# Strided attention's q and k loaded by strips of 36 partitions and turned as blocks of 108 rows, q and k weights split by expert, the last output tile in halves, and a new order of all operations

## The chip, the cores and the metric

The kernel runs on one core of a Trainium2 chip. The metric is the device time of one execution in microseconds, as the median of several runs. Beside it one execution was taken by the hardware profiler; its trace gives the span from the first to the last instruction and what every engine did in it.

## The reference

Sparse attention with eight heads is followed by a mixture of four causal attention experts of which each token uses two. Everything is float32; the weights of q and k of the experts are drawn eight times larger than the listing shows.

```python
# attention: q, k, v are [8 batches, 8 heads, 576, 64]
scores = scale * np.matmul(q, k.transpose(0, 1, 3, 2))
mask_local = (rel >= 0) & (rel < 32)                       # heads 0 to 3
mask_strided = (rel >= 0) & (pos[None, :] % 32 == pos[:, None] % 32)   # heads 4 to 7
attn = softmax(scores where the head's mask holds)
x = heads side by side of attn @ v                          # [8, 576, 512]
# mixture: wq, wk, wv are [4, 512, 64], wo is [4, 64, 512]
logits = x @ w_gate                                         # the two largest experts, softmax of the two
for e in range(4):
    q, k, v = x @ wq[e], x @ wk[e], x @ wv[e]
    a = causal softmax of scale * (q @ k.T)
    out += weight of e (0 where not chosen) * (a @ v @ wo[e])
```

## The kernel before

The work of a batch has two stages. Stage 1 takes two heads at a time, so a batch has two local pairs (heads 0 to 3) and two strided pairs (heads 4 to 7). It loads q, k and v, turns q and k so that the head dimension lies on the partitions (`tp`, then copies `tp_out` out of PSUM into the tile `qkt`), takes the scores (L633 local, L649 strided), masks them, runs a softmax in six steps spread over VectorE, GpSimd and ScalarE, turns the result (L703 or L713), multiplies by v (L743 local, L762 strided), and splits the attention output into a rounded part `xh` and a remainder `xl`. Stage 2 projects these to q, k and v of the experts with three float32r matmuls per product (L913, L925 for the first pair of experts of batch 0, L860 for v), and goes on with causal scores (L971), softmax, transposes (L1070), values (L1109) and the output projection `out_tile` (L1138).

Batches 0 and 1 turn q and k on TensorE; from batch 2 on (`quad`) VectorE does it. For a strided pair of batches 0 and 1, a token's place is 32 j + g with residue g; L506 loads each strip of 11 or 10 residues on 18 partitions (j) with both heads beside each other, q from partition 0 and k from partition 64 of the tile `nat`, and L603 turns pieces of 54 rows, q and k on two halves of the array. `nat` has three buffers, `qkt` two.

The weights are split into a rounded part and a remainder, `hi_w` on ScalarE and `lo_w` on VectorE or GpSimd. For q and k they are loaded and split by slice of 128 inputs, all four experts in one piece, so any projection needs all four pieces of its weight.

The program is a list of operations (`OPS`) with their dependences. A written table decides the rest: `ORDER` is the sequence in which the operations are issued, and so the sequence on every engine's queue; `SECOND` says which operations run on the second of their two possible engines; `FILL` puts filler matmuls ahead of an operation, if a PSUM bank is free then:

```python
for n, i in enumerate(ORDER):
    o = OPS[i]
    e = list(o.eng)[i in SECOND]
    if o.fill and RB.first() is not None:
        bank = RB.tiles[RB.first()]
        for _ in range(o.fill):
            nc.tensor.matmul(bank[:, :128], ident, ident, start=True, stop=True)
    o.fn(e)
```

Five more matmuls, `warm`, stand first on TensorE (L1158). All loads and stores are issued by SyncE's queue in the table's sequence.

Of the kernel before, what the change touches and what calls it, by code (L numbers as in the profile page):

```python
# [20 lines left out]
def attention_moe_kernel(  # L21
# [20 lines left out]
    nc = tc.nc  # L42
# [38 lines left out]
    class Ring:  # L81
# [34 lines left out]
    }  # L116
    ORDER = [
# [1103 lines left out]
```

## Time and profile before

| | before |
|---|---|
| median of 3 runs (lowest to highest) | 439.55 us (439.47 to 440.03) |
| the profiled execution: its time, its span | 439.54 us, 437.8 us |
| TensorE busy | 428.4 us, 98% of the span |
| VectorE, ScalarE, GpSimd busy | 356.3, 268.3, 231.1 us |
| first matmul, first projection (L925), last matmul's copy | 2.57, 42.44, 434.11 us |
| filler matmuls (L304) | 122 records, 18.0 us busy, all before the first projection |
| granted TensorE clock | 1.00 over the span |

Times within the trace count from the start of the span; 1.7 us of the execution's time lie around it. A float32 matmul that is not a transpose has two records, a transpose or a float32r matmul one. A busy TensorE counts fillers as work. An engine that is busy is not for that the one that is waited for: the chain of waits says which was.

### The profile page before, as it was taken

Reading aid. Unit: us, or ns where it says so; the run is one execution under the profiler, and the core shown is the slowest. Engines: PE = TensorE matmul, PEld = TensorE weight load, DVE = VectorE, ACT = ScalarE, POOL = GpSimd, SP = SyncE. Lnnn points to the kernel's source line nnn. Section 1 sums busy time; section 2 is a strip of 40 time slices with the busy share of each in tenths; the row PEclk is TensorE's granted clock in tenths of the full one; section 3 lists DMA queues with packets and bytes.
Section 4 is the critical chain, followed back from the end, with each engine's and each line's share of the span. In section 5 each row is a group of like instructions: output and inputs, shape, how many; then the busy total and the mean of one; then the engine's idle time right before and its main releaser. Section 6 shows DMA issues by size and latency. Waiting matters only on the chain.

```text
span 437.8 us, 18842 instructions
## 1 busy us (share of the span) xinstructions
PE 428.4 (98%) x7588; PEld 376.6 (86%) x7588; DVE 356.3 (81%) x1140; ACT 268.3 (61%) x852; POOL 231.1 (53%) x375
## 2 busy tenths in 40 slices
PE   7999999999999999999999999999999999999996
PEld 6998998997789889788889788998789988998675
DVE  4798999899998896998889888896888888458750
ACT  4486647857676475566665378725577377557743
POOL 4164782678717842843819633679026771417720
PEclk9999999999999999999999999999999999999999
DMA  7665754766635634653256236355241030011113
GB/s 193 155 147 145 144 113 97 148 105 109 125 61 96 122 98 79 137 115 81 51 106 122 76 90 137 73 104 111 73 118 40 1 108 1 26 24 53 70 53 120
DMA packets 156271, 41.87 MB, mean 96 GB/s; under 512 B 145976, under 2 KB 149432, under 8 KB 156184
## 3 DMA queue, kind: packets, MB, share of 16 engines
q1 hardware_dynamic: 156184, 40.67, 42.0%
q8 instruction: 60, 0.98, 0.9%
q14 instruction: 27, 0.22, 0.2%
HBM read 31.20 MB, written 9.44 MB: 93 GB/s over the span
## 4 chain that ended last, share of the span: by engine, by line
PE 86%; DVE 5%; ACT 4%; DMA 2%; issue 1%; SPq 1%; POOL 1%; DVEq 0%; POOLq 0%; ACTq 0%
PE bank L913 19%; PE bank L1138 11%; PE bank L860 10%; PE bank L1109 10%; PE bank L1070 6%; PE bank L971 6%; PE bank L743 3%; PE bank L762 3%; PE bank L304 2%; PE bank L633 2%; PE bank L1008 2%; PE bank L649 2%; PE bank L713 2%; PE bank L925 2%; PE bank L823 1%
## 5 line engine op out<-in xcount | busy, mean ns | idle before, releaser
L1043 POOL TENSOR_SCALAR p<-p,st,wt 128x384 f32<-128x384 f32 (+3 forms) x128 | 77.3, 622 | 42.0 <-DVE st L1034 22.9
L983 ACT ACTIVATE p<-p,st 128x256 f32<-128x256 f32 (+3 forms) x128 | 72.1, 568 | 9.1 <-DVE st L978 8.9
L978 DVE CUSTOM_DVE_ANT_0 p<-bank,m_cau 128x128 f32<-128x128 f32 (+3 forms) x128 | 57.5, 481 | 3.1 <-PE bank L971 2.9
L526 DVE STREAM_TRANSPOSE qkt<-nat 128x576 f32<-128x576 f32 x48 | 47.7, 1004 | 3.5 <-DMA nat<-in_k_dram 3.1
L1109 PE MATMUL bank<-th,vs 128*64 128x192 f32 (+4 forms) x512 | 49.2, 338 | 0.0
L341 ACT COPY th<-bank 128x256 f32<-128x256 f32 (+2 forms) x104 | 40.6, 431 | 12.2 <-PE bank L1070 11.7
L676 POOL TENSOR_TENSOR p1l<-p1l,st 128x640 f32<-128x640 f32 (+1 forms) x18 | 20.7, 1154 | 49.6 <-DVE st L674 40.0
L1109 PEld LDWEIGHTS bank<-th,vs 128*64 128x64 f32 x512 | 34.1, 137 | 14.2 <-issue 7.0
L934 ACT CAST qk<-bank 128x288 fp32r<-128x288 f32 x64 | 25.0, 399 | 30.6 <-PE bank L913 22.8
L725 ACT CAST xh<-bank 128x160 fp32r<-128x160 f32 (+4 forms) x112 | 28.9, 321 | 22.4 <-PE bank L743 9.9
L727 DVE TENSOR_TENSOR xl<-bank,xh 128x160 fp32r<-128x160 f32 (+4 forms) x112 | 31.6, 323 | 6.4 <-ACT xh L725 5.7
L860 PE MATMUL bank<-wh_v,xh 128*128 128x260 f32 x128 | 36.5, 285 | 0.3 <-DVE qkl L936 0.3
L913 PE MATMUL bank<-xh,wh_k 128*128 128x288 f32 x120 | 36.5, 304 | 0.2 <-DVE st L978 0.2
L860 PE MATMUL bank<-wh_v,xl 128*128 128x260 f32 x128 | 36.2, 283 | 0.0
L913 PE MATMUL bank<-xh,wh_q 128*128 128x288 f32 x120 | 36.2, 302 | 0.0
L860 PE MATMUL bank<-wl_v,xh 128*128 128x260 f32 x128 | 36.1, 282 | 0.0
L1070 PEld LDWEIGHTS bank<-ident,p 64*128 64x128 f32 x800 | 30.5, 139 | 6.5 <-issue 3.0
L1070 PE MATMUL bank<-ident,p 64*128 64x64 f32 x800 | 35.2, 227 | 0.5 <-DVE pt L341 0.5
L913 PE MATMUL bank<-xl,wh_q 128*128 128x288 f32 x120 | 35.4, 295 | 0.0
L913 PE MATMUL bank<-xl,wh_k 128*128 128x288 f32 x120 | 35.4, 295 | 0.0
L913 PE MATMUL bank<-xh,wl_k 128*128 128x288 f32 x120 | 35.3, 294 | 0.0
L913 PE MATMUL bank<-xh,wl_q 128*128 128x288 f32 x120 | 35.3, 294 | 0.0
(188 smaller groups left out, 1268.0 us busy)
## 6 DMA issues: line engine op xcount, KB each, us to landing
out_dram<-ys SPq DMA_DIRECT2D x32, 256.0 KB
nat<-in_q_dram SPq DMA_DIRECT2D x96, 72.0 KB
nat<-in_k_dram SPq DMA_DIRECT2D x96, 72.0 KB
v<-in_v_dram SPq DMA_DIRECT2D x96, 40.0 KB
v<-in_v_dram SPq DMA_DIRECT2D x48, 54.0 KB
v<-in_v_dram SPq DMA_DIRECT2D x32, 48.0 KB
v<-in_v_dram SPq DMA_DIRECT2D x32, 45.0 KB
out_dram<-ys SPq DMA_DIRECT2D x8, 128.0 KB
```

The lines of the kernel that those rows point to most:

```text
L341: (nc.scalar.copy if e == "ACT" else nc.vector.tensor_copy)(dst, src)
L526: op("tq", {"DVE": 0.66 if local else 1.11}, k0 - 13, lambda e, x=x: nc.vector.transpose(turned(qkt.t, x), raw(x) if local else raw(x).rea ...
L725: op("xh", {"ACT": act(n_) + 0.04 * (not local)}, key, lambda e, s_=s_, x_=x_: nc.scalar.copy(x_(xh.t), s_(xa.t)), r=[xa], w=[xh[u]])
L727: op("xl", {"DVE": dve(n_)}, key + 0.5, lambda e, s_=s_, x_=x_: nc.vector.tensor_sub(x_(xl.t), s_(xa.t), x_(f(xh.t))), r=[xa, xh[u]], w=[x ...
L860: nc.tensor.matmul(vp.t[:, :NV], xx.t[:, t0:t0 + 128], ww.t[:, kt, :], start=i == 0, stop=i == 11)
L913: nc.tensor.matmul(pj.t[:, :HS], ww.t[:, kt, ep * 128:(ep + 1) * 128], xx.t[:, c], start=i == 0, stop=i == 11)
L978: lambda e, sp=sp, p=p, a=a, nk=nk, ci=ci, st=st[ep]: nc.vector.tensor_tensor_reduce(out=p.t[:, a, :nk], in0=sp[a].t[:, :nk], in1=m_cau[:, ...
L983: op("exp2", {"ACT": 0.285 + 0.00084 * nk}, k_ + 1, lambda e, p=p, a=a, ci=ci, nk=nk, st=st[ep]: nc.scalar.activation(p.t[:, a, :nk], p.t[ ...
L1043: lambda e, p=p, a=a, ci=ci, t=t, nk=nk, s_=s_, ep=ep: nc.gpsimd.tensor_scalar(p.t[:, a, :nk], p.t[:, a, :nk], s_.t[:, 20 + ci + a:21 + ci ...
L1070: nc.tensor.transpose(tp[hf].t[:, 64 * c:64 * c + 64], src, ident[r, r])
L1109: nc.tensor.matmul(acc.t[o, c0:c0 + cn], vw, th[ep, a].t[:, s0:s0 + cn], start=j == 0, stop=j == nj - 1, skip_group_check=True)
L1138: nc.tensor.matmul(yp.t[:, :DM], xx.t[:, c0:c0 + 128], ww.t[:, ep, :], start=i == 0, stop=i == 5)
```

## The change

Six things change. (1) The strided q and k of batches 0 and 1 are loaded by three strips on 36 partitions each (both heads below each other), q into the first half of the columns of `nat` and k into the second. (2) They are turned by twelve transposes of 108 rows per pair in place of twenty-four of 54 rows, on the whole array in place of its halves; the four copies of 324 columns per pair write in a pattern of 9 x 2 x 18. Each turned tensor is tracked by itself (q and k apart). (3) The weights of q and k are loaded and split by expert, so the projection of a pair of experts needs two of four pieces. (4) The last full output tile is computed, copied and stored in two halves of 256 columns. (5) The tables `ORDER`, `SECOND` and `FILL` are new throughout; the filler matmuls that are issued go from 61 to 41. (6) The sequence of the first loads is another: of batch 0 one local pair is loaded first and then both strided pairs, where it was both local pairs and then one strided.

```diff
-        0, 1, 2, 44, 45, 8, 3, 13, 6, 5, 10, 14, 4, 87, 7, 9, 46, 11, 15, 12, 49, 88, 18, 19, 202, 51, 52, 181,
+        0, 2, 1, 3, 8, 88, 4, 11, 13, 125, 12, 95, 14, 7, 5, 15, 10, 6, 9, 18, 132, 93, 87, 45, 20, 124, 59, 22,
...
-        8: 5, 13: 6, 18: 7, 51: 1, 56: 3, 76: 1, 89: 4, 92: 5, 96: 1, 124: 4, 131: 2, 148: 4, 208: 2, 218: 1,
-        241: 2, 246: 8, 279: 2, 282: 3, 1132: 2, 1150: 3, 1151: 4,
+        0: 3, 3: 5, 13: 3, 18: 6, 51: 2, 61: 2, 76: 3, 95: 1, 98: 1, 115: 1, 128: 2, 207: 5, 217: 1, 245: 1,
+        250: 1, 255: 1, 315: 2, 1140: 2, 1144: 8, 1145: 1, 1146: 7, 1158: 2, 1159: 6, 1160: 8,
...
+        if name in "qk":
+            for ex in range(E):
+                st = wide[ex // 2][ex % 2]
+                def raw(ex=ex):
+                    return flat(ex // 2)[:, ex % 2 * n:ex % 2 * n + n].rearrange("p (a d) -> p a d", d=D)
+                c = slice(ex * D, ex * D + D)
+                op("load_0", {"SP": 0.5}, k_ + 0.1 * ex, lambda e, ex=ex, raw=raw: nc.sync.dma_start(
+                    raw(), src[ex].rearrange("(a p) d -> p a d", p=128)), w=[st], dmas=[(0.47, 0.71)])
+                op("hi_w", {"ACT": 0.1 + act(n)}, 15 + k_ * 0.1, lambda e, c=c, raw=raw: nc.scalar.copy(hi.t[:, :, c], raw()),
+                   r=[st], w=[hi[ex]])
...
-                    p_ = 64 * x + NJ * r
-                    nc.sync.dma_start(nat.t[p_:p_ + NJ, :22 * D].rearrange("p (h c) -> p h c", h=2)[:, :, :n_], strips(base, 11 * r, n_))
+                    p_, c_ = 2 * NJ * r, 11 * D * x
+                    nc.sync.dma_start(nat.t[p_:p_ + 2 * NJ, c_:c_ + n_], bass.AP(
+                        tensor=base.tensor, offset=base.offset + 11 * r * D, ap=[[STR * D, 2 * NJ], [1, n_]]))
...
-                for g in range(6):
-                    for x in range(2):
-                        r = slice(64 * x, 64 * x + 54)
-                        c = (11 * u + 2 * g) * D
-                        nc.tensor.transpose(tp[x].t[:, 54 * g:54 * g + 54], nat.t[r, c:c + 128], ident[r, r])
+                    r = slice(0, 6 * NJ)
+                    for g in range(3):
+                        c = (11 * x + 6 * u + 2 * g) * D
+                        nc.tensor.transpose(tp.t[:, 108 * g:108 * g + 108], nat.t[r, c:c + 128], ident[r, r])
...
+                op("tp_out", either(324), k0 - 13 + 0.5 * x + 0.2 * u, lambda e, tp=tp, halves=halves: copy(
+                    e, halves(), tp.t[:, :324].rearrange("p (g h j) -> p g h j", h=2, j=NJ)), r=[tp], w=[qkt[x]])
...
-        return [W[nm][i][kt, ep] for i in range(2) for kt in range({"o": E * D // 128}.get(nm, KT))]
+        parts = range(2 * ep, 2 * ep + 2) if nm in "qk" else range(E * D // 128 if nm == "o" else KT)
+        return [W[nm][i][x] for i in range(2) for x in parts]
...
+        cut = 2 if b == B - 1 and t == 3 else 1
+        n_ = DM // cut
+        for h in range(cut):
...
+                    nc.sync.dma_start(out[b, t0:t0 + 128, c], ys.t[:, c])
```

Three places of the new order are shown; a `bank` is a PSUM bank, `qkt_191` and `qkt_193` are the two buffers of the turned q and k, and lines after the change stand 17 to 26 higher.

TensorE at the head of the program, up to the first block of local scores (L633, after the change L653; only its first row stands here), before:

```order
L1158 MATMUL bank_64<-p1l_72 128x256 x5
L304 MATMUL bank_65<-ident 128x128 x5
L574 MATMUL bank_65<-ident,p_169 128x128 x4
L574 MATMUL bank_66<-ident,p_169 128x128 x4
L304 MATMUL bank_67<-ident 128x128 x6
L587 MATMUL bank_67<-ident,p_169 128x128 x2
L574 MATMUL bank_68<-ident,p_170 128x128 x4
L304 MATMUL bank_69<-ident 128x128 x7
L633 MATMUL bank_69<-qkt_191 32x64
```

and after:

```order
L305 MATMUL bank_64<-ident 128x128 x3
L1184 MATMUL bank_64<-p1l_72 128x256 x5
L305 MATMUL bank_65<-ident 128x128 x5
L591 MATMUL bank_65<-ident,p_169 128x128 x4
L591 MATMUL bank_66<-ident,p_169 128x128 x4
L305 MATMUL bank_67<-ident 128x128 x3
L604 MATMUL bank_67<-ident,p_169 128x128 x2
L305 MATMUL bank_68<-ident 128x128
L620 MATMUL bank_68<-ident,nat_179 128x108 x3
L305 MATMUL bank_69<-ident 128x128 x6
L653 MATMUL bank_69<-qkt_191 32x64
```

Three fillers now stand ahead of the warm-up matmuls, and three strip transposes and six fillers stand where four local transposes and seven fillers stood.

VectorE from the mask of the first local pair (L663, then L683) to the end of its softmax sums (L685, then L705), before:

```order
L663 TENSOR_TENSOR p1l_72<-bank_69,m_loc 128x320
L663 TENSOR_TENSOR p1l_72<-bank_70,m_loc 128x320
L674 TENSOR_REDUCE st_205<-p1l_72 128x5 x2
L341 COPY qkt_193<-bank_71 64x64x4 x2
L341 COPY qkt_193<-bank_68 64x64x4 x2
L680 TENSOR_REDUCE st_205<-p1l_72 128x5 x2
L683 TENSOR_REDUCE st_205<-st_205 128x10
L685 RECIPROCAL st_205<-st_205 128x10
```

and after:

```order
L683 TENSOR_TENSOR p1l_72<-bank_70,m_loc 128x320
L694 TENSOR_REDUCE st_205<-p1l_72 128x5
L683 TENSOR_TENSOR p1l_72<-bank_69,m_loc 128x320
L694 TENSOR_REDUCE st_205<-p1l_72 128x5
L342 COPY qkt_193<-bank_64 128x9x2x18
L342 COPY qkt_191<-bank_70 128x9x2x18
L700 TENSOR_REDUCE st_205<-p1l_72 128x5 x2
L703 TENSOR_REDUCE st_205<-st_205 128x10
L705 RECIPROCAL st_205<-st_205 128x10
```

Each half's maximum now follows its mask at once, and two strip copies stand ahead of the sums in place of four copies of a second local pair.

VectorE up to its first remainder of a weight of k (L448, then L444), which the first projection waits for, before:

```order
L341 COPY pt_203<-bank_71 128x324
L674 TENSOR_REDUCE st_207<-p1l_73 128x10
L727 TENSOR_TENSOR xl_219<-bank_68,xh_214 128x128
L727 TENSOR_TENSOR xl_219<-bank_69,xh_214 128x128
L727 TENSOR_TENSOR xl_220<-bank_70,xh_215 128x18x3x6
L341 COPY pt_204<-bank_67 128x324
L341 COPY qkt_191<-bank_68 128x324
L341 COPY qkt_191<-bank_71 128x324
L341 COPY qkt_191<-bank_64 128x324
L448 TENSOR_TENSOR wl_k_265<-th_175,wh_k_264 128x256
```

and after:

```order
L747 TENSOR_TENSOR xl_219<-bank_67,xh_214 128x160
L747 TENSOR_TENSOR xl_219<-bank_66,xh_214 128x128
L694 TENSOR_REDUCE st_205<-p1l_72 128x10
L342 COPY qkt_193<-bank_68 128x9x2x18
L747 TENSOR_TENSOR xl_219<-bank_71,xh_214 128x128
L683 TENSOR_TENSOR p1l_73<-bank_69,m_loc 128x320
L342 COPY pt_203<-bank_64 128x324
L342 COPY qkt_191<-bank_71 128x9x2x18
L444 TENSOR_TENSOR wl_k_265<-th_176,wh_k_264 128x4x64
```

The weight has moved ahead of the second maximum of 640 columns, of one copy of a turned softmax, of two strip copies and of the first strided pair's `xl`.

## Rows read from the trace of the kernel before

**Rows 1.** The profile's page: busy time, share of the span and instructions of each engine.

```profile
...
PE 428.4 (98%) x7588; PEld 376.6 (86%) x7588; DVE 356.3 (81%) x1140; ACT 268.3 (61%) x852; POOL 231.1 (53%) x375
...
```

**Rows 2.** Windows: busy us (instructions) by engine, granted clock, DMA share, GB/s.

```profile
...
9.75:42.11 32.36, 32.21 (x931) 29.57 (x932) 27.46 (x72) 20.17 (x57) 13.21 (x18) 1.00 0.63 153
42.44:434.11 391.67, 388.67 (x6621) 340.48 (x6620) 324.41 (x1025) 243.28 (x786) 213.16 (x334) 1.00 0.41 88
...
```

**Rows 3.** Timeline of TensorE: start us, us, engine, line, operation, shapes, count, idle before.

```profile
...
2.57 4.63 PE L1158 MATMUL bank<-p1l 128*128 128x256 f32 x10 [2.57 <-ACT bank L351]
7.00 1.77 PE L304 MATMUL bank<-ident 128*128 128x128 f32 x10
8.61 1.04 PE L574 MATMUL bank<-ident,p 128*128 128x128 f32 x8
...
22.77 0.95 PE L603 MATMUL bank<-ident,nat 54*128 54x54 f32 x24
...
28.31 1.95 PE L304 MATMUL bank<-ident 128*128 128x128 f32 x16
...
```

**Rows 4.** The same timeline: blocks of scores (L633) and of values (L743), batches 0 and 1.

```profile
...
13.13 0.97 PE L633 MATMUL bank<-qkt 64*32 64x64 f32 x72
...
19.00 0.97 PE L633 MATMUL bank<-qkt 64*32 64x64 f32 x72
...
27.00 1.11 PE L743 MATMUL bank<-pt,v 32*64 32x32 f32 x84
...
30.85 1.15 PE L633 MATMUL bank<-qkt 64*32 64x64 f32 x72
...
34.88 1.11 PE L743 MATMUL bank<-pt,v 32*64 32x32 f32 x84
...
```

**Rows 5.** Chain of work that ended last, in order of time, around the first projection.

```profile
...
42.44 1.99 PE bank L925 x12
44.44 0.74 PE bank L649 x44
...
46.17 3.17 PE bank L913 x24
...
```

**Rows 6.** Groups by line and shape, 9.75 to 42.11: busy us, mean ns, idle before.

```profile
...
L341 ACT COPY qkt<-bank 64x256 f32<-64x256 f32 x20 | 8.3, 421 | 10.0 <-DVE qkt L341 6.6 <-PE bank L574 3.2
L341 DVE COPY qkt<-bank 64x256 f32<-64x256 f32 x12 | 4.9, 424 | 4.6 <-PE bank L574 4.4
...
L676 POOL TENSOR_TENSOR p1l<-p1l,st 128x320 f32<-128x320 f32 x4 | 2.9, 724 | 13.8 <-ACT qkt L341 9.6 <-DVE st L674 4.3
...
L341 DVE COPY qkt<-bank 128x324 f32<-128x324 f32 x5 | 2.2, 472 | 0.0
...
L678 ACT ACTIVATE p1l<-p1l 128x320 f32<-128x320 f32 x4 | 1.9, 468 | 0.0
...
L674 DVE TENSOR_REDUCE st<-p1l 128x10 f32<-128x640 f32 x2 | 1.6, 814 | 0.0
...
```

**Rows 7.** Timeline of VectorE: the sums of the first softmax.

```profile
...
18.84 0.88 DVE L680 TENSOR_REDUCE st<-p1l 128x5 f32<-128x320 f32 x2 [1.29 <-ACT p1l L678]
...
```

**Rows 8.** Windows: loads on 128 partitions alone, and a stretch rich in strips.

```profile
...
3.00:5.00 2.00, 2.00 (x6) 1.55 (x6) 1.76 (x29) 2.00 (x6) 1.70 (x9) 1.00 1.00 349
16.00:19.10 3.10, 3.10 (x52) 2.74 (x56) 1.78 (x5) 2.20 (x6) 1.41 (x2) 1.00 0.60 148
...
```

**Rows 9.** Chain of work: one projection behind 128-row work, one behind scores on quarter tiles.

```profile
...
134.65 1.60 PE bank L913 x12
...
145.49 1.78 PE bank L913 x12
...
```

**Rows 10.** Timeline of all engines: the last three pieces of the program.

```profile
...
433.93 0.59 SPq L1148 DMA_DIRECT2D out_dram<-ys  x1
434.11 0.59 ACT L341 COPY ys<-bank 128x512 f32<-128x512 f32 x1 [0.73 <-PE bank L1138]
434.72 0.44 SPq L1150 DMA_DIRECT2D out_dram<-ys  x1
...
```

More of the change, by code (lines that the diff above doesn't have):

```diff
@@ L418, in load_weights @@
         hi, lo = W[name]
-        eps = (0, 1) if name in "qk" else (0,)
         k_ = first("w" + name)
@@ L430, in load_weights @@
                w=[wide[i][0], wide[i][1]], dmas=[(0.5, 0.2)])
+        if name in "qk":
[8 more added lines that the diff above has]
+                   r=[st], w=[hi[ex]])
+                op("lo_w", {"DVE": 0.1 + dve(n), "POOL": 0.1 + 0.0025 * n}, 15.5 + k_ * 0.1, lambda e, c=c, raw=raw: (
+                    nc.vector if e == "DVE" else nc.gpsimd).tensor_sub(lo.t[:, :, c], raw(), f(hi.t[:, :, c])),
+                   r=[st, hi[ex]], w=[lo[ex]])
+            return
         for kt in range(nk):
@@ L445, in load_weights @@
             op("hi_w", {"ACT": 0.1 + act(n)}, 15 + k_ * 0.1, lambda e, kt=kt, raw=raw: nc.scalar.copy(hi.t[:, kt, :], raw()),
-               r=[st], w=[hi[kt, ep] for ep in eps])
+               r=[st], w=[hi[kt]])
             op("lo_w", {"DVE": 0.1 + dve(n), "POOL": 0.1 + 0.0025 * n}, 15.5 + k_ * 0.1, lambda e, kt=kt, raw=raw: (
                 nc.vector if e == "DVE" else nc.gpsimd).tensor_sub(lo.t[:, kt, :], raw(), f(hi.t[:, kt, :])),
-               r=[st] + [hi[kt, ep] for ep in eps], w=[lo[kt, ep] for ep in eps])
+               r=[st, hi[kt]], w=[lo[kt]])
     NAT = fixed("nat", [128, (11 * 2 + 1) * D], 3, value=lambda t: [t[:, c * D:(c + 1) * D] for c in (10, 21, 22)])
@@ L504, in load_qk @@
                     n_ = (11 if r < 2 else 10) * D
-                    p_ = 64 * x + NJ * r
-                    nc.sync.dma_start(nat.t[p_:p_ + NJ, :22 * D].rearrange("p (h c) -> p h c", h=2)[:, :, :n_], strips(base, 11 * r, n_))
+                    p_, c_ = 2 * NJ * r, 11 * D * x
+                    nc.sync.dma_start(nat.t[p_:p_ + 2 * NJ, c_:c_ + n_], bass.AP(
+                        tensor=base.tensor, offset=base.offset + 11 * r * D, ap=[[STR * D, 2 * NJ], [1, n_]]))
         def strips(base, g0, n_):
             return bass.AP(tensor=base.tensor, offset=base.offset + g0 * D, ap=[[STR * D, NJ], [S * D, 2], [1, n_]])
-        dm = [(0.51, 0.48)] if quad else [(0.44, 1.15)] if local else [(0.34, 0.67)] * 3
+        dm = [(0.51, 0.48)] if quad else [(0.44, 1.15)] if local else [(0.34, 0.45)] * 3
         for x, src in enumerate((q, k)):
@@ L514, in stage1 @@
                 op(*(("load_qk", {"SP": 0.54}, k0 - 30) if b > 1 else ("load_0", {"SP": 0.54}, first("x", b, hp))),
-                   lambda e, src=src, x=x, h=h, y=y: load_qk(src, x, h, y), w=[nat[x]] if quad else [nat], dmas=dm)
+                   lambda e, src=src, x=x, h=h, y=y: load_qk(src, x, h, y), w=[nat] if local and not quad else [nat[x]], dmas=dm)
         def turned(t, x):
@@ L594, in stage1, with tps, halves @@
                    r=[tp], w=[qkt[0], qkt[1]])
-        for u in range(0 if quad or local else 2):
-            tp = [RB.new(f"tp{u}{x}_{n}") for x in "qk"]
-            def tps(e, tp=tp, u=u):
-                for g in range(6):
-                    for x in range(2):
-                        r = slice(64 * x, 64 * x + 54)
-                        c = (11 * u + 2 * g) * D
-                        nc.tensor.transpose(tp[x].t[:, 54 * g:54 * g + 54], nat.t[r, c:c + 128], ident[r, r])
-            op("tp", {"PE": 0.063 * 6}, k0 - 14 + u, tps, r=[nat], w=[*tp, qkt[0], qkt[1]], mode=MR)
-            for x in range(2):
-                c0 = (2 * x + u) * 324
-                op("tp_out", either(324), k0 - 13 + u, lambda e, t_=tp[x], c0=c0: copy(
-                    e, qkt.t[:, c0:c0 + 324], t_.t[:, :324]), r=[tp[x]], w=[qkt[0], qkt[1]])
+        for x in range(0 if quad or local else 2):
+            for u in range(2):
+                tp = RB.new(f"tp{u}{x}_{n}")
+                def tps(e, tp=tp, x=x, u=u):
+                    r = slice(0, 6 * NJ)
+                    for g in range(3):
+                        c = (11 * x + 6 * u + 2 * g) * D
+                        nc.tensor.transpose(tp.t[:, 108 * g:108 * g + 108], nat.t[r, c:c + 128], ident[r, r])
+                op("tp", {"PE": 0.115 * 3}, k0 - 14 + 0.5 * x + 0.2 * u, tps, r=[nat[1], nat[x]][u == 0 or x:], w=[tp, qkt[x]], mode=M128)
+                def halves(x=x, u=u):
+                    t_ = qkt.t[:, 648 * x + 162 * u:]
+                    return bass.AP(tensor=t_.tensor, offset=t_.offset, ap=[list(t_.ap[0]), [NJ, 9], [324, 2], [1, NJ]])
+                op("tp_out", either(324), k0 - 13 + 0.5 * x + 0.2 * u, lambda e, tp=tp, halves=halves: copy(
+                    e, halves(), tp.t[:, :324].rearrange("p (g h j) -> p g h j", h=2, j=NJ)), r=[tp], w=[qkt[x]])
         for h in range(2 if local else 1):
@@ L928, in project @@
                     op("pj", {"PE": 3 * 0.132}, key + step * u + 0.1 * kt, part,
-                       r=[X[b, kt][i][x] for i in range(2) for x in range(4)] + [W[nm][i][kt, 0] for i in range(2)],
+                       r=[X[b, kt][i][x] for i in range(2) for x in range(4)] + wbufs(nm),
                        w=[pj, qk[j, u]], mode=M128)
@@ L1129, in out_tile, with mm, store @@
         c0 = 0 if last else QT[t][0]
-        yp, ys = RB.new(f"yp_{b}_{t}"), YS.new(f"ys_{b}_{t}")
+        ys = YS.new(f"ys_{b}_{t}")
         src = [OF[b // 2, ep] if last else O[b, ep] for ep in range(2)]
         need = [x[i] for pair in src for x in pair for i in ((0, 1) if last else (int(t > 2),))]
-        def mm(e):
-            i = 0
-            for ep in range(2):
-                for xx, ww in split3(src[ep], W["o"]):
-                    nc.tensor.matmul(yp.t[:, :DM], xx.t[:, c0:c0 + 128], ww.t[:, ep, :], start=i == 0, stop=i == 5)
-                    i += 1
-        op("yp", {"PE": 6 * 0.229}, key, mm, r=need + wbufs("o"), w=[yp, ys], mode=M128)
-        op("yp_out", either(DM), key + 0.5, lambda e: copy(e, ys.t, yp.t[:, :DM]), r=[yp], w=[ys])
-        def store(e):
-            t0 = QT[t][0]
-            if last:
-                nc.sync.dma_start(out[b - 1, t0:, :], ys.t[:64, :])
-                nc.sync.dma_start(out[b, t0:, :], ys.t[64:, :])
-            else:
-                nc.sync.dma_start(out[b, t0:t0 + 128, :], ys.t)
-        op("store", {"SP": 0.5}, key + 1, store, r=[ys], dmas=[(0.4, 0.4)] * 2 if last else [(0.4, 0.8)])
+        cut = 2 if b == B - 1 and t == 3 else 1
+        n_ = DM // cut
+        for h in range(cut):
+            yp = RB.new(f"yp_{b}_{t}" + "b" * h)
+            c = slice(h * n_, (h + 1) * n_)
+            def mm(e, yp=yp, c=c):
+                i = 0
+                for ep in range(2):
+                    for xx, ww in split3(src[ep], W["o"]):
+                        nc.tensor.matmul(yp.t[:, :n_], xx.t[:, c0:c0 + 128], ww.t[:, ep, c], start=i == 0, stop=i == 5)
+                        i += 1
+            op("yp", {"PE": 6 * 0.229 / cut}, key + h, mm, r=need + wbufs("o"), w=[yp, ys[h]], mode=M128)
+            op("yp_out", either(n_), key + h + 0.5, lambda e, yp=yp, c=c: copy(e, ys.t[:, c], yp.t[:, :n_]), r=[yp], w=[ys[h]])
+            def store(e, c=c):
+                t0 = QT[t][0]
+                if last:
+                    nc.sync.dma_start(out[b - 1, t0:, :], ys.t[:64, :])
+                    nc.sync.dma_start(out[b, t0:, :], ys.t[64:, :])
+                else:
+                    nc.sync.dma_start(out[b, t0:t0 + 128, c], ys.t[:, c])
+            op("store", {"SP": 0.5}, key + h + 1, store, r=[ys[h]], dmas=[(0.4, 0.4)] * 2 if last else [(0.4, 0.8)])
     wb = RB.new("warm")
```

301 rows, old and new, of tables (ORDER, SECOND) are left out of this document.

## The prediction

> **What bounds the kernel now.** I read the page first: TensorE is busy 98% of the span [rows 1]. The windows split that in two. From the first projection at 42.44 to the last matmul at 434.11 TensorE works 388.67 of 391.67 us [rows 2]: what the change does there is worth only what it takes off TensorE's own work, or part of 3.0 us of idle time. Before 42.44 the same share means little, because fillers count as work. A filler takes 0.24 us (eight in 1.95 us) to 0.35 (five in the first 1.77 us) [rows 3]; 61 of them stand before 42.44, so some 15 to 21 us of that head are TensorE waiting, in effect. The head is paced by a chain from engine to engine: turn, copy, scores, mask, softmax, values, split. In it VectorE works 27.46 of 32.36 us from its first copy to its first weight remainder [rows 2]. So I ask two things: at what time does the new order reach a state with the same TensorE work left, and what does that rest cost now?
>
> Such a state can be read from the order. Before, the first projection that is not cut by head pairs (L913) starts at 46.17 [rows 5]; all transposes of q and k, four local and four strided blocks of scores, two of each of values and 18 projection matmuls of L925 are done then. In the new order exactly the same has been issued ahead of the first such matmul, and what is left is the same matmul for matmul (4606 against 4612, six more for the halved tile).
>
> **The change part by part.**
>
> *The transposes.* Twenty-four of 54 rows took 0.95 us per strided pair [rows 3]. Nothing in the trace has 108 rows; eight of 128 took 1.04, 0.13 each, and by columns 108 would take 0.11, so twelve take 1.3 to 1.6. I take 1.3: +0.35 us per pair on TensorE, hidden in a head that has fillers to spare; uncovered it would be 1.4 in all. The copies keep their number and size. Their split pattern costs between a plain copy of 324 columns (472 ns) and the 424 ns per 256 columns of the copies that already write spread (537 for 324) [rows 6]: 0 to 0.07 us each, 0.5 us on VectorE at most. I take 0.03.
>
> *The loads.* A stretch of loads on 128 partitions moved 349 GB/s at a DMA share of 1.00, one rich in strips of 18 partitions 148 at 0.60 [rows 8]: strips use the engines badly. Thirty-six partitions are bounded by no gain and by the full rate. I take no term: two tensors now land first, and in the chain below each strip has landed before TensorE's turn for it. [...]
>
> *The head, step by step*, with the new order's rows and the durations of rows 6 (copy 0.42, exponent 0.47, GpSimd subtraction or product 0.72, reduction of 640 columns 0.81):
> 1. Three fillers go ahead of the warm-up: 0.6 to 1.0 us, I take 0.8. The first transposes start at 9.4 (8.61 [rows 3]).
> 2. The ten copies are split six and four over VectorE and ScalarE, so the first local pair is ready at 12.5; but three transposes and six fillers stand ahead, and its scores start at 13.1 as before (13.13 [rows 4]).
> 3. The maxima follow their masks one by one, and two strip copies replace four local ones ahead of the sums. GpSimd and ScalarE start earlier, and the sums start at 16.8. Before, VectorE waited 1.29 us for ScalarE there and started at 18.84 [rows 7].
> 4. Both strided blocks of scores come next, at 16.9 and 19.35. The second local block waits for eight copies on ScalarE: 22.6 (19.00 [rows 4], but no strided block was done then).
> 5. The first local values 23.5 (27.00), the third local block of scores 27.05 (30.85) [rows 4].
> 6. The second local values wait for VectorE's transpose behind a softmax that began late: 32.0 (34.88 [rows 4]); TensorE has three fillers and then 3 us of nothing.
> 7. From 32.0 VectorE has 15 pieces to the first weight remainder, 6.3 us by their rows: 38.3 to 38.5. TensorE has the second local values, a block of local scores, 21 strip transposes, two turned softmaxes, a block of strided values and three fillers, and waits for the copy of a turned softmax: first projection at 39.15 (42.44 [rows 5]).
> 8. Six matmuls, a filler, a value block, two strided score blocks (0.74 each [rows 5]) and twelve matmuls: the state of equal rest at 44.15 (46.17): **-2.0 us**.
>
> The weights by expert have no price of their own in this: as many pieces of the same size are split. Before, the cut projections of k took their four pieces one after the other; now two pieces serve all of it, so a projection can follow two remainders, and in step 7 VectorE's first one still decides. What is moved behind, a second reduction of 640, a mask, a copy and two remainders, VectorE does in its 40 to 44 us.
>
> *The rest.* Its matmuls are the same. The order changes TensorE's tile shape 170 times in it, 166 before; a projection behind quarter tiles took 1.78, behind full tiles 1.60 [rows 9]. Four changes cost 0 to 0.7 us, I take **+0.4**. The idle 3.0 us are waits that the old order has; the new one has its own, and nothing here tells how many. I keep 3.0, with bounds of 1 and 6.
>
> *The tail.* The last copy of 512 columns takes 0.59 us and its store is issued at 434.72 [rows 10]. Half of it takes about 0.37, but SyncE's queue is occupied to 434.52 by the store before [rows 10], and has two issues of 0.44 to make then: the last starts at 434.96, 0.24 later, with half the bytes. Between -0.4 and +0.3, I take 0; six more short matmuls cost **+0.05**.
>
> Sum: -2.0 + 0.4 + 0.05 = -1.55 us. The profiled execution took 439.54 us, the median is 439.55, so I make it against the median: **438.0 us**, -0.35%. Within 0.2% (0.9 us) a measurement of this kernel tells no change.
>
> **The rivals.**
>
> *The head is shorter still.* If TensorE never waited in it, 21 fillers fewer give 5.0 us, two blocks moved behind 1.5, dearer transposes cost 1.4: first projection at 37.3, and equal rest at 42.3. For it: the planner set its fillers where it saw waits, and sees fewer. Against it: the 3 us of step 6 follow from the queues. That is 1.85 us more than in step 8: half of it gives 437.1, all of it 436.1, and with the middle's waits cut from 3.0 to 1 at the same time 434.1.
>
> *The lead is given back.* VectorE is nearly full after the head too: 324.41 of 391.67 us [rows 2], and TensorE 2 us ahead asks for copies 2 us earlier. Then waits in the middle grow from 3.0 to about 4.6, and the time is 439.5. For it: VectorE gains little by the change (one operation fewer in the whole program). Against it: five copies of local pairs move to ScalarE, which has room.
>
> [...]
>
> *The change does little:* if the strips arrive no earlier and each hand-over costs 0.1 us more than I let it, step 8 comes at 45 to 46, and the time is 439 to 440.
>
> **How the numbers follow.** My forecast, 436.8 to 438.7, has 0.35; a shorter head, 434.5 to 436.8, 0.23; the lead given back or never won, 438.7 to 440.4, 0.20; slower by clock or by new waits in the middle, 0.22. The likeliest time is 438.0. The range leaves out the lower part of the second case (all of the shorter head and fewer waits at once) and the upper half of the last: 435.0 to 441.2. Faster by more than 0.2%: 0.58; within: 0.20; slower: 0.22.
>
> **What would show it.** [...] I am wrong if the head ends where it did, or if the middle gains or loses more than 3 us of waits.

## The result and the profile after

The changed kernel takes 435.72 us (median of four runs, 434.97 to 437.27); four runs of before beside it have 439.51. The ratio is 0.9895, interval 0.9866 to 0.9924: 3.8 us faster, where 1.55 were forecast. Repeated in a later series (experiment 3) it took 436.55 us (nine runs) beside 440.16 (27 of before), ratio 0.9933, interval 0.9912 to 0.9953. Ratios leave out executions over 1.5% above the fastest of the same kernel: two of six in experiment 4, one of thirteen in 9, one of those 27.

The page of after, its first part, beside [rows 1]:

```profile
span 433.3 us, 18662 instructions
...
PE 421.8 (97%) x7506; PEld 370.8 (86%) x7506; DVE 356.5 (82%) x1139; ACT 270.3 (62%) x857; POOL 230.5 (53%) x372
```

TensorE has 6.6 us less to do, of which 4.5 are the 20 fillers fewer (18.0 us busy before, 13.5 after); the other engines have within 2 us what they had. The timeline of TensorE shows the head of after, beside [rows 3 to 5]:

```profile
2.67 1.62 PE L305 MATMUL bank<-ident 128*128 128x128 f32 x6 [2.67 <-ACT bank L352]
4.08 3.12 PE L1184 MATMUL bank<-p1l 128*128 128x256 f32 x10
...
8.16 1.04 PE L591 MATMUL bank<-ident,p 128*128 128x128 f32 x8
...
11.87 0.97 PE L653 MATMUL bank<-qkt 64*32 64x64 f32 x72
...
22.49 1.11 PE L763 MATMUL bank<-pt,v 32*64 32x32 f32 x84
...
28.14 0.50 PE L620 MATMUL bank<-ident,nat 108*128 108x108 f32 x3 [0.70 <-DMA nat<-in_q_dram]
28.48 0.85 PE L305 MATMUL bank<-ident 128*128 128x128 f32 x6
30.54 1.10 PE L763 MATMUL bank<-pt,v 32*64 32x32 f32 x84 [1.21 <-DVE st L703]
...
33.02 1.34 PE L620 MATMUL bank<-ident,nat 108*128 108x108 f32 x12
...
37.90 0.38 PE L946 MATMUL bank<-xh,wh_k 128*128 128x288 f32 x1
...
42.82 0.29 PE L934 MATMUL bank<-xh,wh_q 128*128 128x288 f32 x1
```

The last row is the state of equal rest. In the same view of before it stands at 46.01 (the chain has 46.17). So the head ends 3.2 us earlier. What follows is read from windows, from that state to the last matmul's end, first of before, then of after (engines as in [rows 2]):

```profile
46.01:434.07 388.06, 385.09 (x6560) 337.30 (x6558) 321.43 (x1016) 239.76 (x775) 210.89 (x332) 1.00 0.40 87
```

```profile
42.82:429.60 386.78, 383.89 (x6566) 336.18 (x6564) 321.57 (x1017) 239.95 (x775) 208.71 (x326) 1.00 0.41 88
```

The rest is 1.3 us shorter in these two profiles, although TensorE's idle time in it is the same (2.97 and 2.89). The end of the program, timeline of all engines, beside [rows 10]:

```profile
429.63 0.37 ACT L342 COPY ys<-bank 128x256 f32<-128x256 f32 x1 [1.11 <-PE bank L1164]
429.75 1.03 SPq L1176 DMA_DIRECT2D out_dram<-ys  x2
```

From the last matmul's end to the end of the span are 3.66 us, before 3.76.

### The profile page after: what moved, and what is told of

It reads as the page before. It is cut to its first block, busy times and chain, and to the rows that moved or that the text cites. A ratio compares the mean times of both kernels' runs of the same rounds, so it can differ in the third digit from the quotient of the medians.

```text
span 433.3 us, 18662 instructions
## 1 busy us (share of the span) xinstructions
PE 421.8 (97%) x7506; PEld 370.8 (86%) x7506; DVE 356.5 (82%) x1139; ACT 270.3 (62%) x857; POOL 230.5 (53%) x372
## 4 chain that ended last, share of the span: by engine, by line
PE 84%; DVE 8%; SPq 2%; ACT 2%; issue 1%; DMA 1%; POOL 1%; DVEq 0%; POOLq 0%; ACTq 0%
PE bank L934 19%; PE bank L1164 12%; PE bank L1130 10%; PE bank L881 9%; PE bank L992 6%; PE bank L1091 6%; PE bank L763 3%; PE bank L782 3%; PE bank L653 3%; PE bank L669 2%; PE bank L305 2%; DVE qkt L543 2%; PE bank L733 2%; PE bank L1029 2%; SPq L569 1%
## 5 line engine op out<-in xcount | busy, mean ns | idle before, releaser
L1064 POOL TENSOR_SCALAR p<-p,st,wt 128x256 f32<-128x256 f32 (+3 forms) x128 | 77.2, 615 | 37.4 <-DVE st L1055 20.1
L1004 ACT ACTIVATE p<-p,st 128x128 f32<-128x128 f32 (+3 forms) x128 | 72.0, 566 | 10.7 <-DVE st L999 10.4
L342 ACT COPY th<-bank 128x384 f32<-128x384 f32 (+2 forms) x103 | 41.0, 440 | 19.3 <-PE bank L1091 14.2
L747 DVE TENSOR_TENSOR xl<-bank,xh 128x128 fp32r<-128x128 f32 (+4 forms) x112 | 32.1, 323 | 5.9 <-ACT xh L745 5.5
L957 DVE TENSOR_TENSOR qkl<-bank,qk 128x288 fp32r<-128x288 f32 x64 | 27.0, 442 | 9.4 <-ACT qk L955 7.8
L1091 PE MATMUL bank<-ident,p 64*128 64x64 f32 x800 | 34.2, 226 | 0.0
```

Of the source, the lines that this page charges most:

```text
L342: (nc.scalar.copy if e == "ACT" else nc.vector.tensor_copy)(dst, src)
L747: op("xl", {"DVE": dve(n_)}, key + 0.5, lambda e, s_=s_, x_=x_: nc.vector.tensor_sub(x_(xl.t), s_(xa.t), x_(f(xh.t))), r=[xa, xh[u]], w=[x ...
L1004: op("exp2", {"ACT": 0.285 + 0.00084 * nk}, k_ + 1, lambda e, p=p, a=a, ci=ci, nk=nk, st=st[ep]: nc.scalar.activation(p.t[:, a, :nk], p.t[ ...
L1064: lambda e, p=p, a=a, ci=ci, t=t, nk=nk, s_=s_, ep=ep: nc.gpsimd.tensor_scalar(p.t[:, a, :nk], p.t[:, a, :nk], s_.t[:, 20 + ci + a:21 + ci ...
L1091: nc.tensor.transpose(tp[hf].t[:, 64 * c:64 * c + 64], src, ident[r, r])
```

## The experiments

Times are medians; each ratio is to the kernel before on the same chip. "Rise" is the moment at which the trace's record of the granted clock begins; ahead of it the records of the warm-up in after start 0.43 us apart, behind it 0.22. The lower level of the granted clock is 0.50 (after, window 432.40 to 433.20). Lines of the tables are cut to the entries that change.

**1. Without the three fillers ahead of the warm-up; 2. before with three.**

```diff
-        0: 3, 3: 5, 13: 3,
+        3: 5, 13: 3,
```
```diff
-        8: 5, 13: 6, 18: 7, 51: 1,
+        0: 3, 8: 5, 13: 6, 18: 7, 51: 1,
```

> The kernel after without the three fillers ahead of the five warm-up matmuls; all else as after. Theory 1 (the three fillers let the granted clock rise earlier: the warm-up took 2.96 us behind them, 4.43 us before): without them the warm-up takes 4.4 us again, the first transposes start at 8.6 in place of 8.16 or later, the state of equal rest comes about 0.5 us or more after 42.82, and the time is 0.4 to 1.3 us over that of after (435.7). Rival (the clock rises at a moment of its own, whatever is issued first, and differs from run to run): warm-up and first transposes fall anywhere between the two, and the time is that of after within 0.5 us. Rival by my forecast (the fillers cost 0.8 us): 434.9.

> The kernel before with three fillers ahead of its warm-up matmuls, all else as before. Theory 1: the warm-up takes about 3.0 us behind the fillers in place of 4.43, first transposes at 8.2 in place of 8.61, and 438.3 to 439.1 in place of 439.5. Rival (fillers cost what they take, 0.8 us at the lower level of the clock): first transposes at 9.4 and 440.3. Rival (the clock's moment is chance): 439.5 within 0.5.

The first took 437.01 us beside 440.55 (0.9935, 0.9908 to 0.9962), the second 441.91 (1.0028, 1.0003 to 1.0053). Timeline of TensorE, the first transposes, of 1 and then of 2:

```profile
7.69 1.04 PE L591 MATMUL bank<-ident,p 128*128 128x128 f32 x8
```

```profile
9.08 1.04 PE L574 MATMUL bank<-ident,p 128*128 128x128 f32 x8
```

The rise was at 6.12 and 7.56, against 8.03 in before and 5.70 in after: it doesn't follow the fillers. With it, all four first transposes fall into place: count the time until the rise half and the time behind it whole, and TensorE had 3.31 (before), 3.35 (1), 3.98 (after) and 3.97 us (2) of work ahead of them. The fillers cost 0.65 us; theory 1 falls, and the rival of a moment of its own fits. That 0.8 us come back without them, the third forecast, did not show: by their ratios 1 and after (0.9933 in experiment 3) are equal.

**3. After itself once more**, in the series of 6 to 8.

> The kernel after itself, unchanged, as the measure for the others of this series. Theory 1 (the moment at which the granted clock rises, 5.70 us in the first profile of after and 6.1 to 8.7 in the other profiles, is not of the kernel's making): this profile rises at some other moment between 5.5 and 9, the first transposes start half of that difference later than 8.16, and the state of equal rest as much later than 42.8. Rival (the new order makes the rise earlier): again 5.7 and 8.16. The work of TensorE behind the state of equal rest, without idle time and slow stretches, is 383.8 to 384.2 again (385.0 to 385.5 with the old order).

436.55 us. The rise came at 8.64. Timeline of TensorE, then the window from the equal rest on:

```profile
9.61 1.04 PE L591 MATMUL bank<-ident,p 128*128 128x128 f32 x8
...
39.44 0.38 PE L946 MATMUL bank<-xh,wh_k 128*128 128x288 f32 x1
```

```profile
44.37:430.97 386.60, 383.96 (x6566) 336.12 (x6564) 321.79 (x1017) 239.78 (x775) 208.70 (x326) 1.00 0.40 87
```

The equal rest stands at 44.37: 34.76 us behind the first transposes, as in the first profile of after (34.66). Theory 1 holds: the two heads differ by little but the rise. The rest takes 386.60 us.

**4. After with strips of 18 partitions and 54-row transposes; 5. before with strips of 36 and 108-row blocks.**

```diff
-                    p_, c_ = 2 * NJ * r, 11 * D * x
+                    p_ = 64 * x + NJ * r
...
-                    r = slice(0, 6 * NJ)
-                    for g in range(3):
+                    r = slice(64 * x, 64 * x + 54)
+                    for g in range(6):
```

> The kernel after, its order and all else, but with the old strips (18 partitions, both heads beside each other) and 54-row transposes of each tensor. Theory 2 (the order makes the head shorter, the strips take no part on the path): each pair's transposes are 0.35 us shorter and hidden, the state of equal rest stays at 42.8 within 0.4, the time at 435.3 to 436.1. Rival (the wider strips arrive earlier and the order lives on that): TensorE waits for strips where it waits 0.70 us now, the head gains 1 to 2 us, and the time is 436.7 to 438.

> The kernel before, its order and all else, but with strips of 36 partitions and blocks of 108 rows. Theory 2 (no part on the path): 439.5 to 440.0, first projection at 42.4 to 42.8. Rival (strips arrive earlier and that alone shortens the head): first projection at 41 to 42, time 438 to 439.

Both are slower than either kernel: 446.45 us (1.0113, 1.0082 to 1.0145) and 447.91 (1.0153, 1.0118 to 1.0188). No theory had that. The profiled execution of 4 took 452.38 us, the slowest of its six; where the clock fell in the others is not on record (mean clock 0.977 to 0.994). In it the twelve strips of batch 0 have landed at 17.45 us, in after at 13.01 (last semaphore event of the twelfth), and TensorE waits for them (timeline, then windows by stage; the column behind POOL is the granted clock):

```profile
17.58 0.55 PE L619 MATMUL bank<-ident,nat 54*128 54x54 f32 x6 [1.44 <-DMA nat<-in_q_dram]
```

```profile
20.00:30.00 10.00, 10.00 (x250) 9.20 (x254) 5.97 (x14) 4.92 (x13) 2.68 (x4) 0.71 0.91 198
...
40.00:50.00 10.00, 8.96 (x142) 8.24 (x144) 7.30 (x17) 4.92 (x14) 5.58 (x7) 0.64 0.65 133
```

Behind that wait, and again behind waits near 40, the clock falls to the lower level, for 6.8 and 10.2 us, and once more for 6.8 us at a wait inside a block of scores at 108. Its transposes also cost more than in before, with q and k turned one after the other (30 in 1.50 us, where 24 took 0.95), so not all of the loss is the loads'. In 5 the strips come earlier too (the twelfth at 15.68, in before at 19.18), and nothing uses it, since the order asks for them when it did. What it loses begins inside a block of scores (timeline, then window):

```profile
39.40 0.63 PE L637 MATMUL bank<-qkt 64*32 64x64 f32 x18 [2.24 <-issue]
```

```profile
40.00:50.00 10.00, 10.00 (x181) 9.12 (x181) 5.14 (x13) 3.13 (x11) 0.73 (x1) 0.56 0.70 154
```

For 2.24 us TensorE waits for nothing that the profile shows, and then the clock has the lower level for most of 10 us (0.56 over the window). Its rest takes 391.3 us, with 4.6 us of such waits. So what 5 loses is not traced to the strips. More on such waits stands at the end.

**6. After without any filler.** `FILL` is empty.

> The kernel after with no filler matmul at all (41 are issued in after); the five warm-up matmuls stay. Theory (the fillers hold the granted clock up through the waits of the head): the clock falls to the lower level at least once between 10 and 45 us, each fall for 3.4 to 10 us costs half of that, and the time is 438 to 445. Rival (fillers only take time from TensorE's queue): clock 1.00, the head ends as in after or up to 1 us earlier, 434.5 to 436.

441.10 us (1.0031, 1.0007 to 1.0055): all of the gain is gone. Windows with the clock's column, then the timeline of TensorE:

```profile
20.00:30.00 10.00, 6.16 (x209) 5.15 (x201) 7.62 (x23) 8.04 (x24) 5.64 (x8) 0.83 0.70 197
30.00:40.00 10.00, 9.50 (x251) 8.49 (x251) 7.65 (x22) 6.54 (x22) 5.01 (x7) 0.66 0.62 164
```

```profile
23.27 0.74 PE L761 MATMUL bank<-pt,v 32*64 32x64 f32 x34 [2.01 <-issue]
...
30.50 1.56 PE L761 MATMUL bank<-pt,v 32*64 32x32 f32 x84 [1.87 <-DVE st L701]
```

It falls right behind the first of these waits and within the second. The theory held, in all twelve executions: mean clock 0.973 to 0.992, where after has 0.99 to 1.0. Two things limit it. The first of the two waits lies inside a block of values, where after has no filler either, and ends with no engine. And the falls explain only part of the loss: the equal rest comes at 45.98, 1.6 us later than in experiment 3, while the rest takes 389.7 us, 3.1 more, at the upper level (the two falls of the head make up the profile's mean clock of 0.988), where after has no fillers to take away.

**7. After with the last tile in one piece.**

```diff
-        cut = 2 if b == B - 1 and t == 3 else 1
+        cut = 1
```

> The kernel after with the last full output tile in one piece (one product of 512 columns, one copy, one store), all else as after. My step on the tail (no gain from halving, bounds -0.4 to +0.3 us, and 0.05 for six more matmuls): the time of after within 0.3 us, and 3.7 us from the last matmul to the end of the span in both. Rival (halving hides a copy and half a store): 0.4 to 0.8 us slower than after, at the end of the program alone.

436.87 us (0.9936, 0.991 to 0.9962), after in the same series 436.55; 3.61 us behind the last matmul. No price outside the intervals, as forecast.

**8. After with a short warm-up.**

```diff
-        0: 3, 3: 5, 13: 3,
+        13: 3,
...
-        for _ in range(5):
+        for _ in range(2):
             nc.tensor.matmul(wb.t[:, :256], ones[:, :128], ones, start=True, stop=True)
```

> The kernel after with two warm-up matmuls in place of five and without the three fillers ahead and the five behind them, all else as after. Theory (the head is a chain whose start everything follows; the warm-up stands in front of it): the first transposes start at 4.5 to 5 us, when their loads have landed, in place of 8.16, at the lower clock; the first scores at 9 to 10 in place of 11.87; from then the strips of q and k, the last of the first twelve landing at 13.0, take part of it back: equal rest 1 to 2.5 us earlier, 433.2 to 434.7. Rival (without the warm-up the clock rises later or falls again in the head): first scores at 10 to 12, a granted clock under 1.00 behind 10 us, 436 to 442.

437.49 us (0.9948, 0.9922 to 0.9975). The timeline:

```profile
4.47 1.94 PE L591 MATMUL bank<-ident,p 128*128 128x128 f32 x8
...
9.48 0.97 PE L653 MATMUL bank<-qkt 64*32 64x64 f32 x72
...
13.10 0.47 PE L620 MATMUL bank<-ident,nat 108*128 108x108 f32 x3 [1.11 <-DMA nat<-in_q_dram]
```

The chain starts 3.7 us earlier and the lead shrinks to 0.3 us: with the rise at 7.10 the equal rest is at 43.25, where after, by its own two profiles, would have it near 43.5. TensorE now waits for strips, 1.11, 0.88 and 0.62 us. The warm-up covers loads. The theory misses; the time lies in the rival's range, but not by its cause: the first scores come at 9.48 and the clock keeps the upper level (mean 0.999).

**9. The new head with the old rest; 10. the old head with the new rest.** The table is cut at the state of equal rest; the operations that are left stand in the other kernel's order, on its engines.

The piece of 9's table at the cut:

```diff
-        1157, 1137, 187, 183, 171, 184, 382, 294, 384, 295, 1188, 228, 229, 265, 1184, 190, 258, 194, 1160, 42,
+        294, 384, 295, 1138, 378, 172, 194, 1146, 258, 190, 1181, 1177, 350, 122, 296, 1153, 265,
```

> The kernel after up to its first undivided projection (the state of equal rest), and from there on all operations in the order and on the engines of before. Theory 3 (the rest became 1.3 us shorter by its own order, the head 2 to 3 by its own): the state of equal rest as in after (42.8 to 44.6 by the moment of the clock's rise), then 388.1 us to the last matmul, and 2.0 to 2.6 us less than before. Rival (the order of the rest is worth nothing by itself, the shorter rest comes of the state in which the new head leaves it): rest 386.8, and 3.3 to 3.8 us less than before.

> The kernel before up to its first undivided projection, and from there on all operations in the order and on the engines of after (the last tile in one piece). Theory 3: equal rest at 46, then 386.8 us, and 1.0 to 1.6 us less than before. Rival (the new order of the rest lives on the lead of the new head): new waits of TensorE, 388 us or more, and the time of before or worse.

440.40 us (0.999, 0.9962 to 1.0017) and 441.68 (1.0032, 1.0003 to 1.006): 9 misses both theories on the time, 10 comes out as its rival said. At the seam of 10 TensorE waits 1.18, 0.35 and 0.28 us for weights that the old head has not split yet (timeline):

```profile
48.06 0.40 PE L937 MATMUL bank<-xh,wh_q 128*128 128x288 f32 x1 [1.18 <-ACT wh_q L457]
```

In 9, whose profiled execution was the slowest of thirteen (445.97 us), the clock falls once in the head and twice in the rest (mean 0.984). Without these falls 9's rest, counted from the same state, is 389.0 us, nearer to the old order's 388.1 than to the new one's 386.7. But 2.7 us of it are two waits that end with no engine (us in total, times, longest):

```profile
PE bank L793 <- issue: 2.7, 2, 1.4
```

The first undivided projection stands behind six more matmuls there, which I add. So 9 doesn't show that the time of the rest comes with its order; without such waits, old and new order don't differ (next section). 10 shows that the new rest needs weights that its own head has split.

**11. After with eight more fillers in its two longest waits.**

```diff
-        76: 3,
+        76: 8,
...
-        250: 1, 255: 1, 315: 2,
+        250: 1, 255: 1, 287: 3, 315: 2,
```

> The kernel after with eight more fillers in the two longest waits of its head: three ahead of the strip transposes that wait 0.70 us for a strip at 28.1, and eight in place of three ahead of the second local values that wait 1.21 us for VectorE at 30.5. Theory (in about half of the runs of after the granted clock falls to the lower level behind these waits, mean clock 0.992 to 0.996, for 3.4 to 7 us): the mean clock is 0.998 or more in nearly all runs, and the median is 0.5 to 1.5 us under that of after (3.6 less than before), so 4.1 to 5.1 less than before. Rival (the fillers come too late in the queue or hold the values up): 3.2 to 3.7 less than before, no fewer falls.

437.96 us (0.9944, 0.9921 to 0.9966). The falls are gone (mean clock 0.998 to 1.0 in its runs, 0.992 to 1.0 in those of 3), but the time is 2.2 us under before, where the theory had 4.1 to 5.1 and the rival 3.2 to 3.7. A new wait has come in (timeline):

```profile
36.70 0.59 PE L733 MATMUL bank<-ident,p1s 64*128 64x64 f32 x12 [1.19 <-POOL p1l L696]
```

Rise at 7.05, equal rest at 44.74, 1.2 us later than after would have it: holding the clock by these fillers gives nothing.

**12. After with the weights of q and k by slice of 128 inputs.** TensorE's order is the same.

```diff
-        if name in "qk":
+        if False:
...
-        parts = range(2 * ep, 2 * ep + 2) if nm in "qk" else range(E * D // 128 if nm == "o" else KT)
+        parts = range(E * D // 128 if nm == "o" else KT)
```

> The kernel after with the weights of q and k loaded and split by slice of 128 inputs, as in before; TensorE's order is the same to the last matmul, and one pair of split operations stands earlier, where a projection needs it. Theory (by-expert pieces have no price of their own): first projection and equal rest as in after within 0.5 us, and 3.2 to 4.0 less than before. Rival (the new head rests on needing two pieces of four): the projections wait for more remainders, equal rest 1 to 2.5 us later, and 1.0 to 2.6 less than before.

436.79 us (0.993, 0.9899 to 0.9962): as after, by its ratio. The new head does not rest on the split by expert.

No version beat after: 1, 7 and 12 are equal to it within their intervals, 8 and 11 lie 0.5 to 0.7 us above by their ratios, with intervals that overlap.

## Why the prediction was right and where it was wrong

The sign and the mechanism of the head were right; the size of the whole was not. Its steps, forecast, first profile of after, and second profile (experiment 3):

| step | forecast | after | again |
|---|---|---|---|
| 1 first transposes | 9.4 | 8.16 | 9.61 |
| 2 first local scores | 13.1 | 11.87 | 13.32 |
| 3 sums | 16.8 | 15.60 | 17.05 |
| 4 strided scores | 16.9, 19.35 | 15.74, 18.21 | 17.18, 19.66 |
| 4 second local scores | 22.6 | 21.59 | 23.04 |
| 5 first local values | 23.5 | 22.49 | 24.41 |
| 6 second local values | 32.0 | 30.54 | 32.02 |
| 7 first projection | 39.15 | 37.90 | 39.44 |
| 8 equal rest | 44.15 | 42.82 | 44.37 |

From the first transposes to the equal rest I forecast 34.75 us; they took 34.66 and 34.76. What moved the whole column was the moment of the clock's rise, 5.70 and 8.64: half of their difference is 1.47, the columns differ by 1.44 to 1.55, once by 1.92. Step 1 gave the fillers 0.8 where they cost 0.65, and took the rise of before's one profile (8.03) for fixed. Set to that rise, the head of after is 1.9 to 2.0 us shorter than that of before (half of the shift in the rise added to 42.82, to 44.37, against 46.01); step 8 said 2.0. So the 42.82 of the first profile, 1.3 us ahead of the forecast, is the luck of an early rise.

**The step that failed is the rest**: +0.4 for four more shape changes, idle time kept at 3.0. I had 388.4 us; it took 386.78 and 386.60, so -1.3 to -1.5 in place of +0.4. Of the 3.0 us by which the first profiled execution (434.97) undercut my 438.0, 1.6 are here, and the first profile's early rise makes nearly all of the remainder; of the 1.6 of the second (436.36) it is all. Adding up the distances from the start of one matmul record to the next, from the equal rest on, tells where (the two lines of the q and k projections counted as one line):

| from one matmul to the next | before | after | again |
|---|---|---|---|
| same line of code | 338.1 | 335.0 | 335.3 |
| another tile shape (166, 170 times) | 34.9 | 35.7 | 35.1 |
| another line, same shape | 14.7 | 15.8 | 15.9 |

The shape changes cost +0.2 to +0.8, so the +0.4 was sized rightly. What I left out is the time inside blocks of like matmuls: 2.8 to 3.1 us less. In before three waits show there, in its timeline:

```profile
178.03 0.75 PE L649 MATMUL bank<-qkt,nat 64*54 64x54 f32 x41 [0.54 <-DVE ol L1122]
...
211.33 0.52 PE L1070 MATMUL bank<-ident,p 64*128 64x64 f32 x9 [0.46 <-DVE pt L341]
...
319.69 0.32 PE L762 MATMUL bank<-pt,v 54*64 54x54 f32 x4 [0.78 <-issue]
```

The first two end with VectorE, the third with nothing that the profile shows. The visible idle time inside blocks is 1.83 us in before, 0.49 and 0.68 in after. The other 1.7 us don't show as idle, and their cause is open.

Nor is it shown that the gain belongs to the new order. From the same state on, with half of each fall of the clock taken off, all profiles have (us, in the sequence of the first column; "issue" waits are those of 0.18 us or more that end with no engine and no load):

| profiles | rest | "issue" waits in it | what is left |
|---|---|---|---|
| old rest: before, 2, 5, 9 | 388.1, 388.0, 391.3, 389.0 | 0.8, 1.5, 4.6, 3.1 | 387.3, 386.4, 386.7, 385.9 |
| new rest: after, 3, 1, 7, 12 | 386.8, 386.6, 387.9, 386.6, 387.1 | none | the same |
| new rest: 4, 6, 8, 11 | 388.1, 389.7, 387.6, 387.5 | 2.6, 2.2, 0.8, 0.9 | 385.5, 387.6, 386.8, 386.6 |
| new rest, old head: 10 | 389.2 | 1.7 | 387.5 |

What is left is the same for both orders, 385.9 to 387.3 and 385.5 to 387.9. The orders' rests differ by how much of these waits they have: always some with the old order, none in five of nine profiles of the new order behind its own head, and up to 2.6 us in the other four. Whether the new order has fewer of them by its making, or by chance in the two profiles that I went by, no experiment decides. Head, rest and tail of the first two profiles (2.0, 1.3 to 1.5, 0.1) come to 3.4 to 3.6 of the 3.6 to 3.8 us that the medians differ by.

The other steps:

- *Transposes.* Twelve of 108 rows take 1.34 us (1.3 forecast); the copies that write split patterns 480 ns on VectorE, 8 more than plain ones (30 forecast).
- *Loads, no term.* TensorE waits once for a strip, 0.70 us at 28.14, ahead of a longer wait for VectorE (1.51 us for one in the profile of experiment 1). But no term does not mean no worth: in experiment 4 the new order without the wider strips stands in a wait of 1.44 us for them, and the twelfth strip has landed at 17.45 us where it was 13.01.
- *Weights by expert, the halved tile:* nothing outside the intervals, by 12 and 7.
- *A shorter head* (rival): the first profile's 42.82 looks like it, but was the early rise. *The lead given back*: VectorE is as busy as before in the rest (321.6 us, 321.4), and its idle time did not grow (2.89 us, 2.97). *The change does little*: no.
- *Slower by clock* (with new waits, 0.22): the clock does fall in the head. The profile of experiment 7 has the lower level from 31.0 to 37.8, from the gap of step 6 on, and two of the first four runs of after have a mean clock of 0.996 and 0.99. A fall of 3.4 or 6.8 us at 0.50 costs half of that, 1.7 or 3.4 us. That chance, and the range up to 441.2, were my estimate: no row of before has a fall behind 9.75, and the thirteen runs of after lie at 434.97 to 438.35. Without fillers (6) the head's gain is just gone (equal rest at 45.98, before 46.01); with late strips (4) more is lost.

## What to carry to other kernels

A head that is paced by engine-to-engine hand-overs could here be forecast to a tenth of a microsecond from the new queue order and the old durations, but only from a start that is itself read from more than one profile. Judge a new order's long, full part by more than the engine's tile changes and its idle time in one profile: waits inside blocks of short matmuls came to as much as the whole gain (0 to 4.6 us), and they come and go between profiles of one order. Loads, order and fillers of a tuned head are one thing: either half of this change alone lost more than the whole gains (4 and 5).

## What the runs showed of the hardware

The granted clock rose at 5.70 to 8.70 us in fourteen profiles of kernels whose TensorE starts at 2.57 to 2.67, with no tie to the work in between that I can see; it alone moves the time by up to 1.5 us, half of that range. In experiment 8 it rose, at 7.10, while transposes, fillers and two warm-up matmuls were all that TensorE had done.

Waits "issue" inside blocks of short matmuls go with the pieces that a queue called "instruction" moves. The page of after, third part:

```profile
q8 instruction: 59, 0.97, 0.9%
```

These are 59 pieces of 16 KB (58 to 60 in the other profiles). The waits of 2.24 (experiment 5), 2.01 (6) and 0.78 us (before, at 319.69) each end 1.3 to 1.5 us behind the end of such a piece. So do the others: in the fourteen profiles there are 33 "issue" waits of 0.18 us or more inside blocks of like matmuls, 27.5 us in all, and every one ends 1.2 to 1.8 us behind the last such piece, though only 8% of the time lies there; of 30 waits inside blocks that end with an engine or a load, five do. That TensorE waits for these pieces is argued from this match; no run took them apart, so what sets their moment, and why most pieces bring no wait, stays open.
